# Transposing 64 rows at a time in both halves of the array: a fused windowed-attention and soft-MoE kernel on one Trainium2 core

## The chip, the core and the metric

The kernel runs as one program on one core of a Trainium2 chip. The metric is the device time of one execution, in microseconds (us). The core has five engines that each work through their own instruction queue in order: PE (TensorE: matrix products, with weight loads shown as an engine of their own, PEld), DVE (VectorE), ACT (ScalarE), POOL (GpSimd) and SP (SyncE, which here only issues DMA). PE writes to PSUM, which DVE and ACT read; POOL works on SBUF alone.

## What is computed

Attention with a causal window of 128 positions plus 4 sink positions, then a soft mixture of experts on its output. All data are float32.

```python
# q, k, v: (4 batches, 8 heads, 768 positions, 64)
keep = is_sink | ((rel >= 0) & (rel < 128))          # rel = query position - key position, 4 sinks
a = softmax(where(keep, q @ k.T / 8, -1e9))
x = (a @ v)  laid out as (3072, 512)                 # batch and position, head and dim
logits = x @ phi                                     # (3072, 32): 8 experts of 4 slots
d = softmax(logits, over the 3072 rows)              # dispatch
slot_input = d.T @ x                                 # (32, 512)
slot_out[e] = relu(slot_input[e] @ w1[e]) @ w2[e]    # w1: 512x1024, w2: 1024x512 for each expert
c = softmax(logits, over the 32 slots)               # combine
out = c @ slot_out
```

## The kernel before

**Jobs.** The attention is cut into 12 jobs of 256 positions of one batch (`jobs`: 4 batches, `j` = 0 to 2), all 8 heads at once. Heads lie in pairs: a column block of 128 holds two heads of 64, so `a` = 0 to 3 numbers four pairs, and a "quad" is two pairs. `i` numbers the two blocks of 128 positions of a job, `odd` the two halves of 64 positions in each block. A unit of softmax (`softmax`, `tl` = 0 to 3 in a job) is one quad and one half.

**The steps of a job.** k and q are loaded by DMA (`load`, tile `first_76`) and transposed on PE (`prep`, into `kt` and `qt`). `softmax` makes the scores in tiles of 64x64 of the array into a two-bank PSUM tile `s`; DVE masks and takes the maximum, ACT takes the exponentials into one of three buffers `pts`, POOL divides. `weights_transposed` transposes them into `xws`; `sinks_transposed` does the same for the sink columns. POOL cuts the transposed weights by the window (`select`). `values` multiplies with v into `xt` (features by positions, in `first_77`), `natural` transposes `xt` back to positions by features (`xnb`, also in `first_77`). `Moe.tokens` makes the dispatch logits and adds to the running softmax over rows.

**A transposition** is a product of the data as stationary operand with the identity (`c.ident`): in the profile a weight load (LDWEIGHTS) and a MATMUL `w<-ident,...`. The helper `transpose` does four parts of 128x128 into one PSUM bank, and one copy by ACT or DVE takes the 512 columns out. A job has ten such groups: two for k, two for q, four for the weights and two for `natural`, 40 parts in all.

**PSUM.** There are four single banks of kind `w` (tiles `w` in the profile) and two two-bank tiles of kind `s`.

**Logits.** `tokens` makes them in two steps: `pairs` (four products 32x256 with `phi`, one for each pair of heads, side by side in four column strips of the array), a copy to `lp` (tile `spare`), and `logits` (four products with `c.slot`, which adds the four strips).

**The order of the work** comes from `Plan`: each step is added with a key, the engines that may do it, a guessed time, what it reads and writes, and the shape of array tile it uses (`mode`). `Plan.order` takes for the engine that is free first the ready step with the lowest key, prices a change of mode on PE, and hands out the PSUM banks. The keys come from the table `CFG` (plus 4 for each job). The order is fixed when the program is built; `copy` steps marked "AV" go to ACT or DVE by that same plan. Nearly all instructions of the attention are recorded by one helper, line 127.

**After the attention** comes `finish` (the last steps of the dispatch softmax), then `tail`: the expert products with w1 and w2 (32 weight tiles of 1 MB, 17 of them loaded during the attention, the rest as buffers come free), and the output.

Of the kernel before, what the change touches and what calls it, by code (L numbers as in the profile page):

```python
# [8 lines left out]
F32 = mybir.dt.float32  # L9
# [10 lines left out]
P = 128  # L20
# [120 lines left out]
class Plan:  # L141
# [19 lines left out]
    def add(self, key, eng, time, fn, r=(), w=(), new=None, last=None, mode=(128, 128)):  # L161

        self.steps.append((key, eng, time if isinstance(time, tuple) else (time,) * len(eng), fn,
                           tuple(r), tuple(w), new, last))
        self.modes.append(mode)

    def order(self):
# [3 lines left out]
        for i, (_, eng, _, _, r, w, new, last) in enumerate(steps):  # L171
# [13 lines left out]
            if new is not None:  # L185
                opener[new["name"]] = i
# [17 lines left out]
        while len(order) < len(steps):  # L204
            best = None
            for e, o in todo.items():
                at, t0 = [], 1e9
                for i in o:
                    t = max(free[e], ready[i])
                    new = steps[i][6]  # L210
                    if new is not None:

                        n = len(banks[new["kind"]])
                        if n == 0 or n == 1 and new["kind"] == "w" and not later.get(i, done) <= done:
                            continue
                        t = max(t, min(banks[new["kind"]])[0])
                    at.append((t, i))
                    t0 = min(t0, t)
# [15 lines left out]
            if new is not None:  # L234
                b = min(banks[new["kind"]])
                banks[new["kind"]].remove(b)
                new["bank"] = b[1]
# [12 lines left out]
    def issue(self):  # L250
        order = sorted(self.order())
        end = max(t for t, _, i, e in order if e == "P" and self.steps[i][0] < self.IDLE)
        for t, _, i, e in order:
# [3 lines left out]
            if new is not None:  # L257
                pool, shape, _ = self.pools[new["kind"]]
                new["tile"] = pool.tile(shape, F32, name=new["kind"])
# [18 lines left out]
class Moe:  # L278
# [6 lines left out]
    def __init__(self, nc, c, keep, work, pools, B):  # L285
# [4 lines left out]
        self.spare = keep.tile([P, 256], F32, name="spare")  # L290
# [15 lines left out]
    def tokens(self, plan, keys, b, j, x, xn, blocks):  # L306
# [17 lines left out]
        if both:  # L324

            A, lp = plan.psum(), self.lp
# [6 lines left out]
            plan.add(next(k), "P", 0.45, pairs, r=xs + ["phi"], w=[A["name"]], new=A, mode=(128, 32))  # L333
            plan.add(next(k), "AV", (0.27, 0.34), lambda e: (nc.scalar.copy if e == "A" else nc.vector.tensor_copy)(
                lp, A["tile"][:, 0:256]), r=[A["name"]], w=["lp"], last=A)
# [6 lines left out]
            plan.add(next(k), "P", 0.23, logits, r=["lp"], w=[L["name"]], new=L, mode=(128, 32))  # L342
        else:
            next(k), next(k)

            def logits(e):
                for a in range(4):
                    for g in range(4):
                        nc.tensor.matmul(L["tile"][32 * g:32 * g + 32, 0:P], lhsT=c.phi[:, a, :],
                                         rhs=xt[:, a, x[blocks[0]]], start=(a == 0), stop=(a == 3))  # L350

            plan.add(next(k), "P", 1.2, logits, r=xs + ["phi"], w=[L["name"]], new=L)
# [65 lines left out]
    def finish(self, plan, keys):  # L418
# [11 lines left out]
        swap, slots, sel = self.si.rearrange("p k s -> p (k s)"), self.spare[:, 0:P], self.sel  # L430

        def selectors(e):
            iv, sv = (x.rearrange("p (h i s) -> p h i s", h=2, i=2) for x in (c.ident, swap))
            for i in range(2):
                nc.vector.tensor_copy(sv[:, :, i], iv[:, :, 1 - i])
            nc.vector.reduce_sum(sel, c.ident.rearrange("p (h i s) -> p h s i", h=2, i=2), axis=AX.X)

        plan.add(next(k), "V", 0.6, selectors, w=["fsel"])
# [9 lines left out]
        def inputs(e):  # L448
            for x in range(2):
# [9 lines left out]
        plan.add(next(k), "V", 0.2, lambda e: nc.vector.tensor_copy(  # L459
            slots.rearrange("p (g s) -> p g s", g=4), c.slot.unsqueeze(1).to_broadcast([P, 4, 32])), w=["lp"])  # L460
        plan.add(next(k), "P", 0.25, lambda e: nc.tensor.matmul(Z["tile"][:, 0:1], lhsT=slots, rhs=rz, start=True, stop=True),
                 r=["rz", "lp"], w=["fz"], new=Z)
# [154 lines left out]
class Weights:  # L617
# [9 lines left out]
    def load(self, t):  # L627
# [5 lines left out]
        else:  # L633
# [7 lines left out]
WARM = 8, 10, 24  # L641
PT = 3
CFG = {'prep': [-2.17, -0.88],
       'load': [-3.57, -6.02],
       'v': [-0.18, -0.24],
       'S': -8.73,
       'M': 36.62,
       'E': -5.46,
       'N': 0.31,
       'K0': 2.19,  # L650
       'T': [3.66, 4.85, 4.7, 5.73],
       'K': -1.8,
       'sel': [-6.52, -2.35, 5.2, 5.48],
       'val': [3.28, -5.83, 5.91, 8.36],
       'xn': [2.08, 9.26],
       'tok': [7.72, -14.81, -29.67, 6.11, -4.29, -10.76, 19.93, 9.29, -24.99, 9.79, 6.46, -0.14, -1.55],
       'sm': -17.55,
       'sinks': -36.55,
       'tr': [83.54, 111.89, 84.43, 86.17, 89.04, 123.77, 106.32, 93.21, 89.01, 82.18, 84.62, 87.83, 68.6, 87.87, 106.87,
              85.72, 98.54, 75.2, 46.43, 23.9, 60.71, 53.42, 48.6, 43.21, 70.53, 50.67, 57.49],  # L660
       'w': [14.83, 8.0],
       'fin': [-17.88, 7.56, 0.7, -0.3, 12.51, 20.97, 18.11, 14.38, 20.61, 23.73, 38.59],
       'xn1': [18.28, 18.07],
       'tok1': [4.6, -7.87, -9.73, -4.24, 1.2, -17.1, 3.61, 11.52, -24.18, -0.27, -3.93, 3.34, -6.83]}


def window_path(ctx, tc, c, moe, q, k, v, phi, w1, w2, out):
# [22 lines left out]
    moe.lp = moe.spare[:, 0:256]  # L690
# [21 lines left out]
    QUARTERS, HALVES = (64, 64), (128, 64)  # L712
# [6 lines left out]
    def transpose(key, src, r):  # L719

        h = plan.psum()

        def go(e):
            for a in range(4):
# [22 lines left out]
    def prep(key, n, kind):  # L747

        b, j = jobs[n]
        if kind == 0 and j > 0:  # L750

            add(key, "G", 0.55, lambda e: nc.gpsimd.tensor_copy(ktb[:, :, 0, 4:132], ktb[:, :, 2, 4:132]),
                r=[("kt", 1, 0), ("kt", 1, 1)], w=["kt0"])
        for x in range(2):

            if n == 0:
                h = transpose(key, lambda a, x=x: kqs[kind][:, a // 2, 256 * x + P * (a % 2):256 * x + P * (a % 2) + P],
                              [("kq", kind, i, x) for i in range(2)])
                src, names = "p (i a y) -> p a i y", [(i, x) for i in range(2)]
                a = slice(2 * x, 2 * x + 2)  # L760
                ko, qo = ktb[:, a, 1:3, 4:132], qt[:, a].rearrange("p a (i y) -> p a i y", i=2)
            else:
                h = transpose(key, lambda a, x=x: kqs[kind][:, x, P * a:P * a + P], [("kq", kind, x, y) for y in range(2)])
                src, names = "p (i a y) -> p a i y", [(x, y) for y in range(2)]
                ko, qo = ktb[:, :, 1 + x, 4:132].unsqueeze(2), qt[:, :, P * x:P * x + P].unsqueeze(2)

            def out(e, h=h, src=src, ko=ko, qo=qo):
                s = h["tile"].rearrange(src, i=2 if n == 0 else 1, y=P)
                if kind == 0:
# [457 lines left out]
```

## Time and profile before

| | |
|---|---|
| runs | 257.02, 257.99, 258.00 us; median 257.99 |
| the profiled execution | 257.78 us, with a span of 256.0 us from first to last instruction |
| busy share of the span | PE 89%, PEld 61%, DVE 67%, ACT 56%, POOL 55% |
| granted TensorE clock, mean | 0.964 |
| attention | until 201.12 us, when the first product with w1 starts |
| w1, its transposition, w2 | 201.12 to 232.67 us |
| output | from there to 256.0 us; the last product with the combine weights ends at 243 us |

The first part of the page gives busy time for whole engines over the whole span; the stages differ, so the argument below uses windows of the trace. A PE row gives a start, the time from the first start to the last end, and a count; an fp32 product shows as two MATMULs, a transposition as one.

### The profile page before, as it was taken

How to read it: one execution, taken by the hardware profiler on the slowest of the kernel's cores; microseconds unless marked ns; L12 is line 12 of the kernel's file. 1: busy time of each engine (PE TensorE's matmuls, PEld its weight loads, DVE VectorE, ACT ScalarE, POOL GpSimd, SP SyncE). 2: the span in 40 equal slices, each digit the busy share in tenths (PEclk: the TensorE clock that was granted, in tenths of full speed). 3: DMA queues.
4: the chain of work that ended last, by engine and by line, in shares of the span. 5: the costliest groups of instructions: out<-in, count | busy, mean ns of one | idle time of the engine just before them, and what ended most of it. 6: DMA issues, size and time to landing. Idle time of an engine off the chain costs nothing.

```text
span 256.0 us, 7069 instructions
## 1 busy us (share of the span) xinstructions
PE 229.0 (89%) x2572; PEld 157.2 (61%) x2572; DVE 171.2 (67%) x457; ACT 143.6 (56%) x568; POOL 141.3 (55%) x281
## 2 busy tenths in 40 slices
PE   7778999999999999999999999999699999997800
PEld 7655766776777776676777667677367434345700
DVE  3378968889798979979897997987514513103800
ACT  2367677568596757769675767977615112103700
POOL 1146769587685958669595857869964060000000
PEclk9979999999999999999999999999979999999955
DMA  5699869789899989967999866240609899950995
GB/s 126 133 176 225 227 152 356 186 239 379 162 257 211 343 250 302 276 146 244 256 366 223 235 125 123 59 150 4 206 13 358 300 399 422 414 235 0 399 394 203
DMA packets 84494, 59.34 MB, mean 232 GB/s; under 512 B 76261, under 2 KB 76261, under 8 KB 82917
## 3 DMA queue, kind: packets, MB, share of 16 engines
q1 hardware_dynamic: 84452, 58.83, 76.4%
q8 instruction: 22, 0.36, 0.6%
q14 instruction: 20, 0.16, 0.2%
HBM read 52.53 MB, written 6.29 MB: 230 GB/s over the span
## 4 chain that ended last, share of the span: by engine, by line
PE 66%; DVE 16%; ACT 6%; POOL 5%; issue 3%; ACTq 0%; POOLq 0%; DVEq 0%
PE w L127 47%; PE s L127 17%; DVE wt L127 7%; POOL wt L127 4%; DVE s L127 4%; ACT wt L127 3%; PE w L1179 1%; ACT wt L613 1%; DVE sums L127 1%; DVE first L127 1%; DVE pst L127 1%; DVE spare L127 1%; DVE qt L127 0%; DVE wt L599 0%; ACT wt L598 0%
## 5 line engine op out<-in xcount | busy, mean ns | idle before, releaser
L127 POOL TENSOR_TENSOR wt<-wt 128x528 f32<-128x528 f32 (+1 forms) x96 | 64.3, 673 | 36.3 <-DVE wt L127 22.1
L127 ACT ACTIVATE wt<-s,wt 128x132 f32<-128x132 f32 x192 | 68.8, 386 | 5.6 <-DVE wt L127 5.0
L127 POOL TENSOR_SCALAR_AFFINE_SELECT wt<-wt 128x512 f32<-128x512 f32 x88 | 54.0, 638 | 6.9 <-ACT wt L127 6.4
L127 PE MATMUL w<-wt 128*64 128x128 f32 (+3 forms) x550 | 51.7, 322 | 2.1 <-DVE wt L599 1.5
L127 PE MATMUL s<-wt,qt 64*64 64x196 f32 (+2 forms) x768 | 41.8, 327 | 4.5 <-ACT wt L127 3.7
L127 PEld LDWEIGHTS w<-wt 128*64 128x64 f32 (+2 forms) x550 | 36.7, 143 | 14.8 <-DVE wt L599 2.2
L127 PE MATMUL w<-ident,first 128*128 128x128 f32 x288 | 42.3, 279 | 1.7 <-ACT call L127 1.4
L127 ACT ACTIVATION_READ_ACCUMULATOR wt<-s,wt 128x1 f32 x192 | 42.5, 221 | 0.0
L127 PE MATMUL w<-ident,wt 128*128 128x128 f32 x250 | 38.3, 281 | 1.2 <-POOL wt L127 0.6
L127 PEld LDWEIGHTS w<-ident,first 128*128 128x128 f32 x288 | 32.5, 142 | 7.3 <-issue 2.3
L127 PEld LDWEIGHTS s<-wt,qt 64*64 64x64 f32 x768 | 26.5, 134 | 14.5 <-issue 6.5
L127 DVE TENSOR_REDUCE wt<-s 128x4 f32<-128x528 f32 x48 | 33.9, 707 | 1.7
L127 PEld LDWEIGHTS w<-ident,wt 128*128 128x128 f32 x250 | 28.1, 146 | 11.2 <-issue 3.4
L127 ACT COPY first<-w 128x512 f32<-128x512 f32 x28 | 16.5, 588 | 30.3 <-PE w L127 30.2
L127 ACT COPY wt<-w 128x512 f32<-128x512 f32 x36 | 21.1, 594 | 17.5 <-PE w L127 14.9
L127 DVE COPY_PREDICATED s<-later,s 128x256 f32<-128x256 uint8 x48 | 20.4, 424 | 8.9 <-PE s L127 8.0
L127 DVE COPY wt<-w 128x512 f32<-128x512 f32 x36 | 24.3, 677 | 1.5 <-PE w L127 0.8
L127 DVE COPY first<-w 128x512 f32<-128x512 f32 x20 | 13.7, 684 | 2.0 <-PE w L127 1.9
L127 PE MATMUL w<-wt,si 128*32 128x512 f32 x128 | 13.9, 593 | 0.4 <-DVE si L127 0.4
L127 PE MATMUL s<-wt 128*32 128x512 f32 (+1 forms) x144 | 14.3, 498 | 0.0
L127 DVE MEMSET s<- 64x512 f32 (+1 forms) x16 | 6.2, 385 | 9.5 <-PE s L127 9.1
L127 DVE TENSOR_TENSOR wt<-wt 128x4 f32<-128x4 f32 x48 | 11.2, 232 | 1.8 <-POOL wt L127 0.9
(120 smaller groups left out, 243.9 us busy)
## 6 DMA issues: line engine op xcount, KB each, us to landing
wt<-in_moe_w_dram SPq DMA_DIRECT2D x30, 1024.0 KB, 7.6
wt<-in_v_dram SPq DMA_DIRECT2D x24, 256.0 KB, 3.3
first<-in_q_dram SPq DMA_DIRECT2D x22, 256.0 KB, 3.8
first<-in_k_dram SPq DMA_DIRECT2D x22, 256.0 KB, 4.5
out_dram<-wt SPq DMA_DIRECT2D x5, 1024.0 KB, 5.6
first<-in_moe_w_dram SPq DMA_DIRECT2D x2, 1024.0 KB
out_dram<-wt SPq DMA_DIRECT2D x2, 512.0 KB
first<-in_k_dram SPq DMA_DIRECT2D x4, 128.0 KB, 3.0
```

Source lines behind the costliest of these rows:

```text
L127: return self.tc.keep_in_program_order(f(*args, **kw))
L613: (nc.vector.tensor_copy if i else nc.scalar.copy)(ob[:, n - n0, i], yp)
L1179: nc.tensor.matmul(t[:, 0:P], lhsT=c.ident, rhs=c.ident, start=True, stop=True)
```

## The change

`transpose` now takes eight parts at once and opens two banks. Each part is transposed in two products of 64 rows: rows 0 to 63 in the upper half of the array into the first bank, rows 64 to 127 in the lower half into the second. The stationary operand is 64 rows by 128 columns, the moving one a 64x64 identity. A job has five such units (k, q, the weights of each quad, `natural`) of 16 MATMULs, and again two copies of 512 columns for each. For the very first k and q the units have four parts.

`tokens` makes the logits in one step: 16 products of 32x128 that add up over the four pairs in PSUM. `pairs`, the copy to `lp` and the second product are gone. The units of softmax run quad by quad (`quad, odd = divmod(tl, 2)`), so that the two halves of a quad, which a unit transposes together, follow each other. `Plan` can open several banks for a step. The identity copy for `slots` is made earlier in `finish`. The last filler matmuls (`WARM[2]`) are 64 of 64 columns instead of 24 of 128. All keys of `CFG` have new values.

```diff
-    def transpose(key, src, r):
-        h = plan.psum()
+    def transpose(key, srcs, r):
+        hs = plan.psum(), plan.psum()
         def go(e):
-            for a in range(4):
-                nc.tensor.transpose(h["tile"][:, P * a:P * a + P], src(a), c.ident)
-        add(key, "P", 0.44, go, r=r, w=[h["name"]], new=h)
-        return h
+            for a, src in enumerate(srcs()):
+                for x in range(2):
+                    i = slice(64 * x, 64 * x + 64)
+                    nc.tensor.transpose(hs[x]["tile"][:, 64 * a:64 * a + 64], src[i], c.ident[i, i])
+        add(key, "P", 0.45 if len(r) > 1 else 0.25, go, r=r, w=[h["name"] for h in hs], new=hs, mode=ROWS)
+        return hs
...
-    def weights_transposed(key, n, tl):
-        odd, quad = divmod(tl, 2)
...
-        h = transpose(key, lambda a: pt[:, a, o:o + P], [pn])
...
+    def weights_transposed(key, n, quad):
+        gs = [4 * n + 2 * quad + odd for odd in range(2)]
+        hs = transpose(key, lambda: [pts[g % PT][:, a, o:o + P] for g, o in zip(gs, (0, 4)) for a in range(4)],
+                       [("pt", g % PT) for g in gs])
+        for i in range(2):
+            add(key, *COPY, lambda e, h=hs[i], i=i: copy(
+                e, xws[quad][:, i, 0].rearrange("p h (o y) -> p o h y", o=2),
+                h["tile"].rearrange("p (o h y) -> p o h y", o=2, h=4)),
+                r=[hs[i]["name"]], w=[("xw", quad, i, 0)], last=hs[i])
...
-    def natural(key, n, i):
-        h = transpose(key, lambda a: xt[:, a, P * i:P * i + P], [("xt", i, 0), ("xt", i, 1)])
-        add(key, *COPY, lambda e: copy(e, xnb[i], h["tile"]), r=[h["name"]], w=[("xn", i)], last=h)
+    def natural(key, n):
+        hs = transpose(key, lambda: [xt[:, a, P * i:P * i + P] for i in range(2) for a in range(4)],
+                       [("xt", i, y) for i in range(2) for y in range(2)])
+        for x in range(2):
+            add(key, *COPY, lambda e, h=hs[x], x=x: copy(
+                e, u[:, 0:1024].rearrange("p (i a x y) -> p x i a y", i=2, a=4, x=2)[:, x],
+                h["tile"].rearrange("p (i a y) -> p i a y", i=2, a=4)), r=[hs[x]["name"]], w=[("xn", x)], last=hs[x])
...
-            def pairs(e):
-                for a in range(4):
-                    nc.tensor.matmul(A["tile"][32 * a:32 * a + 32, 0:256], lhsT=c.phi[:, a, :], rhs=xt[:, a, :],
-                                     start=True, stop=True)
...
-            def logits(e):
+        def logits(e):
+            for a in range(4):
                 for g in range(4):
-                    nc.tensor.matmul(L["tile"][32 * g:32 * g + 32, 0:P], lhsT=c.slot, rhs=lp[:, x[g % 2]],
-                                     start=True, stop=True)
+                    nc.tensor.matmul(L["tile"][32 * g:32 * g + 32, 0:P], lhsT=c.phi[:, a, :],
+                                     rhs=xt[:, a, x[g % 2 if both else blocks[0]]], start=(a == 0), stop=(a == 3),
+                                     skip_group_check=True)
...
-        odd, quad = divmod(tl, 2)
+        quad, odd = divmod(tl, 2)
...
-WARM = 8, 10, 24
+WARM = 8, 10, 64
...
-       'xn': [2.08, 9.26],
+       'xn': [-7.99],
```

In the order of the built programs, PE between two score steps of a middle job before (`first_76` holds k and q, `first_77` holds `xt` and `xnb`, `wt` after `ident` is the softmax weights or, twice, the sinks):

```order
L127 MATMUL s<-wt,qt 64x196 x8
L127 MATMUL w<-ident,wt 128x128 x4
L127 MATMUL w<-ident,first_77 128x128 x4
L127 MATMUL w<-ident,wt 128x128 x6
L127 MATMUL w<-ident,first_77 128x128 x4
L127 MATMUL w<-first_77,phi 32x256 x4
L127 MATMUL w<-ident,wt 128x128 x4
L127 MATMUL w<-ident,first_76 128x128 x4
L127 MATMUL w<-spare,slot 32x128 x4
L127 MATMUL s<-wt,qt 64x196 x16
```

All four-part groups here run in one mode of the array, 128x128, with the sinks among them. PE in the changed kernel, around the logits of a middle job:

```order
L127 MATMUL w<-ident,first_76 128x64 x16
L127 MATMUL w<-ident,first_77 128x64 x16
L127 MATMUL w<-first_77,phi 32x128 x16
L127 MATMUL w<-ident,wt 128x64 x16
L127 MATMUL s<-wt,qt 64x196 x16
L127 MATMUL w<-ident,wt 128x128 x2
L127 MATMUL w<-ident,first_76 128x64 x16
L127 MATMUL w<-ident,lt 128x128
L127 MATMUL w<-pst,vsink 128x256 x2
```

Groups of four parts have become units of 16 MATMULs of half the columns; the sinks and the one transposition of `lt` now stand alone in the 128x128 mode, and the two products of the logits, with other work between them before, are one block.

A second place on PE is the last job of a batch in the changed kernel, where the dispatch weights of `tokens` are turned (`lt`) and used (`lb`):

```order
L127 MATMUL s<-wt,qt 64x196 x8
L127 MATMUL w<-ident,wt 128x64 x16
L127 MATMUL w<-ident,wt 128x128 x2
L127 MATMUL w<-ident,lt 128x128
L127 MATMUL w<-first_77,lb 32x256 x4
L127 MATMUL s<-wt,qt 64x196 x8
```

Here `lb` follows `lt` at once. Before, 12 or 16 transpositions stood between the two in the middle jobs:

```order
L127 MATMUL w<-ident,lt 128x128
L127 MATMUL w<-ident,first_76 128x128 x12
L127 MATMUL w<-ident,wt 128x128 x4
L127 MATMUL w<-first_77,lb 32x256 x4
L127 MATMUL w<-pst,vsink 128x256 x2
```

Now nothing stands between them once in three jobs; in the other two jobs a product with v and a score step do.

More of the change, by code (lines that the diff above doesn't have):

```diff
@@ L184, in order @@
             before.append(d)
-            if new is not None:
-                opener[new["name"]] = i
+            for x in new:
+                opener[x["name"]] = i
             for x in r + w:
@@ L233, in order @@
                 todo[x].remove(i)
[L234 to L237, printed above, removed]
+            for x in new:
+                b = min(banks[x["kind"]])
+                banks[x["kind"]].remove(b)
+                x["bank"] = b[1]
             free[e] = end = t0 + times[engs.index(e)]
@@ L323, in tokens @@
         xs = [("xt", b, u) for b in blocks for u in range(2)]
[L324 to L352 removed]
+        def logits(e):
+            for a in range(4):
+                for g in range(4):
+                    nc.tensor.matmul(L["tile"][32 * g:32 * g + 32, 0:P], lhsT=c.phi[:, a, :],
+                                     rhs=xt[:, a, x[g % 2 if both else blocks[0]]], start=(a == 0), stop=(a == 3),
+                                     skip_group_check=True)
+        plan.add(next(k), "P", 0.87, logits, r=xs + ["phi"], w=[L["name"]], new=L, mode=(128, 32))
         key = next(k)
@@ L435, in selectors @@
                 nc.vector.tensor_copy(sv[:, :, i], iv[:, :, 1 - i])
+            nc.vector.tensor_copy(slots.rearrange("p (g s) -> p g s", g=4),
+                                  c.slot.unsqueeze(1).to_broadcast([P, 4, 32]))
             nc.vector.reduce_sum(sel, c.ident.rearrange("p (h i s) -> p h s i", h=2, i=2), axis=AX.X)
-        plan.add(next(k), "V", 0.6, selectors, w=["fsel"])
+        plan.add(next(k), "V", 0.8, selectors, w=["fsel"])
         mm = [("m", 0), ("m", 1)]
@@ new lines, in prep, with out @@
+            hs = transpose(key, src, [("kq", kind, i, y) for i in range(2) for y in quads])
+            for x in range(2):
+                def out(e, h=hs[x], x=x, heads=heads, m=256 * len(quads)):
+                    s = h["tile"][:, 0:m].rearrange("p (i a y) -> p i a y", i=2, y=64)
+                    o = 64 * x
+                    if kind == 0:
+                        copy(e, ktb[:, heads, 1:3, 4 + o:68 + o].rearrange("p a i y -> p i a y"), s)
+                        return
+                    t = qt[:, heads].rearrange("p a (i x y) -> p x i a y", i=2, x=2)[:, x]
+                    if e == "A":
+                        nc.scalar.mul(t, s, D ** -0.5)
+                    else:
+                        nc.vector.tensor_scalar(t, s, D ** -0.5, None, op0=ALU.mult)
+                add(key, "AV", (0.52, 0.65) if n else (0.32, 0.4), out, r=[hs[x]["name"]],
+                    w=[("q" if kind else "kt", x, y) for y in quads], last=hs[x])
@@ L787, in softmax @@
+            if kind == 0 and j == 0:
+                add(key, "G", 0.25, lambda e, a=heads: nc.gpsimd.tensor_copy(
+                    ktb[:, a, 1:3, 0:4], ktb[:, a, 1:2, 4:8].to_broadcast([P, a.stop - a.start, 2, 4])),
+                    r=[("kt", 0, y) for y in quads], w=[("kts", 0, y) for y in quads])
     def softmax(keys, n, tl):
@@ L889, in select @@
         prev, cur = xws[quad][:, i, 0], xws[quad][:, i, 1]
[L890 removed]
+        pn = [("xw", quad, i, 0)]
         add(key, "G", 0.57, lambda e: nc.gpsimd.affine_select(
@@ L974, in window_path @@
         end = "1" if n == N - 1 else ""
-        for i in range(2):
-            natural(t(O["xn" + end][i]), n, i)
+        natural(t(O["xn" + end][0]), n)
         moe.tokens(plan, [t(x) for x in O["tok" + end]], b, j, half, xnb, (0, 1))
@@ L999, in window_path @@
     for quad in range(2):
-        add(100.0, "D", 3.0, lambda e: weight(), w=[("xw", quad, i, 1) for i in range(2)] + [
-            ("xw", quad, i, 0, x) for i in range(2) for x in range(2)])
+        add(100.0, "D", 3.0, lambda e: weight(), w=[("xw", quad, i, x) for i in range(2) for x in range(2)])
     for n in range(9):
```

138 lines of the change are left out of this document (53 added, 85 removed).

## Prediction

> **What bounds the kernel now.** I read the busy shares first, then the table of windows, then the waits of each engine in the steady part.
>
> ```profile
> span 256.0 us, 7069 instructions
> PE 229.0 (89%) x2572; PEld 157.2 (61%) x2572; DVE 171.2 (67%) x457; ACT 143.6 (56%) x568; POOL 141.3 (55%) x281
> ```
>
> To find the steady period I took the first product with `phi` of two jobs nine jobs apart, and the window between them (busy us of PE, PEld, DVE, ACT, POOL).
>
> ```profile
> 39.26 0.42 PE L127 MATMUL w<-first,phi 128*32 128x256 f32 x4
> 170.30 0.42 PE L127 MATMUL w<-first,phi 128*32 128x256 f32 x4
> 39.26:170.30 131.04, 128.92 (x1588) 93.09 (x1584) 114.84 (x297) 93.11 (x390) 96.90 (x184) 1.00 0.85 237
> ```
>
> 131.04 / 9 = 14.56 us for a job, in which PE is busy 14.32, DVE 12.76, ACT 10.35, POOL 10.77. PE is idle 0.24 us a job, and its only rows in the list of waits for that window (us in all, times, longest) are the first two here; the longest of DVE and ACT follow:
>
> ```profile
> PE w L127 <- ACT call L127: 1.4, 3, 0.5
> PE w L127 <- DVE wt L127: 0.5, 1, 0.5
> ...
> DVE s L127 <- PE s L127: 9.7, 16, 1.2
> ...
> ACT first L127 <- PE w L127: 21.6, 13, 2.5
> ```
>
> DVE waits for scores and ACT for products, both from PE. So the attention is bound by PE, and a shorter PE job shortens the kernel as long as DVE, at 12.76 of 14.56, can follow. After the attention nothing that the change touches is left:
>
> ```profile
> 201.12 13.94 PE L127 MATMUL w<-wt,si 128*32 128x512 f32 x128 [0.38 <-DVE si L127]
> 235.96 8.21 SPq L614 DMA_DIRECT2D out_dram<-wt  x7
> ```
>
> 55 us from the first row to the end of the span stay as they are.
>
> **Transpositions, the main term.** What a group costs on PE is read from start to start:
>
> ```profile
> 66.18 0.89 PE L127 MATMUL s<-wt,qt 64*64 64x196 f32 x16
> 67.01 0.66 PE L127 MATMUL w<-ident,wt 128*128 128x128 f32 x4
> 67.50 0.60 PE L127 MATMUL w<-ident,first 128*128 128x128 f32 x4
> 67.94 0.82 PE L127 MATMUL w<-ident,wt 128*128 128x128 f32 x6
> 68.59 0.60 PE L127 MATMUL w<-ident,first 128*128 128x128 f32 x4
> 69.12 0.64 PE L127 MATMUL w<-first,phi 128*32 128x256 f32 x8
> 69.69 0.66 PE L127 MATMUL w<-ident,wt 128*128 128x128 f32 x4
> 70.18 0.60 PE L127 MATMUL w<-ident,first 128*128 128x128 f32 x4
> 70.71 0.43 PE L127 MATMUL w<-spare,slot 128*32 128x128 f32 x8
> 71.07 1.56 PE L127 MATMUL s<-wt,qt 64*64 64x196 f32 x32
> ```
>
> Inside one mode four transpositions take 0.44 us (67.50 to 67.94), so 0.109 for one, or 0.85 ns a column. 40 parts a job cost 4.36 us. The scores row shows what array halves are worth: 16 products of 196 columns at 0.85 ns would be 2.67 us one after the other; 66.18 to 67.01 is 0.83 with the change of mode. So four 64x64 tiles stream at once, two of them row halves, and the new form should run its two halves at once too. A pair then streams 64 columns, 64 x 0.85 = 0.055 us. Each product also needs its own weight load of 128 columns, and the question is whether that fits:
>
> ```profile
> L127 PEld LDWEIGHTS w<-ident,first 128*128 128x128 f32 x288 | 32.5, 142 | 7.3 <-issue 2.3 <-ACT call L127 2.1 <-DVE wt L127 1.3
> L127 PEld LDWEIGHTS w<-first,phi 128*32 128x32 f32 x96 | 1.9, 108 | 2.1 <-issue 1.0 <-ACT wt L127 0.5 <-ACT first L127 0.3
> L127 PEld LDWEIGHTS w<-lt,acc 128*128 128x128 f32 x4 | 0.5, 190 | 0.0
> ```
>
> An ordinary load of 128 columns takes 190 ns, one of 32 columns 108: 82 ns for 96 columns, again 0.85 ns a column, so 109 ns for 128 and a fixed part of 81. A load for a transposition takes 142, so its columns take about 61 ns. The pitch of a pair is the larger of 55 and 61. Bounds: 55 if the load hides wholly, 109 if a 64-row load goes at the ordinary rate or the two halves load in turn (122). I take 60, since the row is that of a transposition. A unit of eight pairs: 0.48 us against 8 x 0.109 = 0.87; five units: 5 x 0.39 = 1.95 us saved a job.
>
> The Trainium skill ("TensorE: Matmul & The Clock Gate", section "LDWEIGHTS (loading the stationary operand)") says that a load takes its columns divided by 1.2 per ns and that the rows don't matter: 107 ns for 64 rows by 128 columns. By that rule a unit would take 8 x 107 = 0.86 us and nothing is saved. The trace agrees for ordinary loads (109) and not for those of transpositions (61).
>
> **Changes of mode.** 69.12 to 69.69 is 0.57 for two rounds of 256 columns, 0.44 by 0.85 ns; 70.71 to 71.07 is 0.36 for 0.22. So a change costs about 0.14 us. Counted over three middle jobs in the order, there were 39 and are now 44: +5/3 x 0.14 = +0.23 us a job.
>
> **Logits.** Before: 0.44 + 0.22 = 0.66 us of streaming. Now 16 products, two MATMULs each, four at a time: 8 rounds of 128 columns, 0.87. +0.21 a job. The copy goes from the vector engines:
>
> ```profile
> L127 DVE COPY spare<-w 128x256 f32<-128x256 f32 x10 | 4.1, 413 | 0.0
> L127 DVE COPY wt<-w 128x512 f32<-128x512 f32 x36 | 24.3, 677 | 1.5 <-PE w L127 0.8
> L127 ACT COPY wt<-w 128x512 f32<-128x512 f32 x36 | 21.1, 594 | 17.5 <-PE w L127 14.9 <-PE s L127 2.5
> ```
>
> **PE sum.** 14.32 - 1.95 + 0.23 + 0.21 = 12.81 us a job, -1.51.
>
> **Can the others follow?** The copies keep number and size (512 columns, 677 on DVE and 594 on ACT), but the new order gives DVE 47 instead of 65 of the large ones and no `spare`, ACT 93 instead of 79. DVE loses 18 x 0.677 + 10 x 0.413 = 16.3 us in all and takes 2.3 of small copies from ACT, ACT gains 14 x 0.594 = 8.3 and gives up 1.4: DVE 11.6, ACT 10.9, POOL 10.8 a job. At a period of 13.2 DVE is at 88%, as it is now, but ACT goes from 71% to 83% and POOL from 74% to 82%. PE will wait more often. One place is sure: where `lb` follows `lt` at once. The last such chain shows its length (PE, then ACT, then PE):
>
> ```profile
> 185.49 0.33 PE L127 MATMUL w<-ident,lt 128*128 128x128 f32 x1 [1.91 <-ACT lt L127]
> 185.85 0.21 ACT L127 COPY lb<-w 128x64 f32<-128x64 f32 x1 [0.42 <-PE w L127]
> 186.12 0.88 PE L127 MATMUL w<-first,lb 128*32 128x256 f32 x8
> ```
>
> 0.63 from start to start, less the 0.11 of the transposition: 0.5 bare, once in three jobs, 0.17 a job. A unit now needs two of four banks at once and both copies before they are free; I add 0.15 a job for that, between nothing (now hidden) and 0.3 at each of five units (half a copy). Idle goes from 0.24 to 0.56: period 13.37, -1.19 us a job, 12 jobs -14.3.
>
> **The ends.** The last job's chain loses `pairs`, copy and second product (0.57 + 0.4 + 0.36 with waits about 1.4) and gets one block (0.87 + 0.14): -0.4 to -0.8. At 187 us PE ran slow after an idle stretch, which the window of these 8 us (granted clock 0.79, the third number from the end) and the same work 3 us later show:
>
> ```profile
> 184.00:192.00 8.00, 6.43 (x53) 4.23 (x55) 1.75 (x4) 1.92 (x7) 5.47 (x14) 0.79 0.07 18
> 187.65 2.99 PE L127 MATMUL w<-wt 128*64 128x256 f32 x24
> 191.01 1.96 PE L127 MATMUL w<-wt 128*64 128x256 f32 x24
> ```
>
> The fillers may now cover it (-1.0) or not; I count -0.3. Costed at nothing: the DMAs keep their number, size and place (17 weight tiles between the loads of the jobs), and a load of q or k lands in 3.8 or 4.5 us (last column) and is needed a job later:
>
> ```profile
> first<-in_q_dram SPq DMA_DIRECT2D x22, 256.0 KB, 3.8
> first<-in_k_dram SPq DMA_DIRECT2D x22, 256.0 KB, 4.5
> ```
>
> If SP held one up, PE would wait at the next unit of k, at most some 4 us once. The earlier `slots` copy lies on DVE beside a PE that is still in the attention. Sum: 257.8 - 14.3 - 0.9 = 242.6; the profiled execution and the median of the runs (257.99) are 0.2 apart. I say 242.5 us.
>
> **Rivals.** *The weight load sets the pitch* (the other side). If a 64-row load runs at 109 ns, a unit takes 0.87 as before, and the job gains 0.44 us of PE work from modes and logits: 12 x 0.44 = +5.3, less 0.9 at the end, 262; with the two halves in turn, at 122, 12 x (0.44 + 0.52) - 0.9 gives 268. It decides from a pitch of (4.36 - 0.44) / 40 = 98 ns a pair upward. For it: `w<-lt,acc`, the only row with 128 columns of weights to 64 of moving, has the full 190. Against: that is no transposition, and 288 transpositions have 142. The rule of the Trainium skill named above ("TensorE: Matmul & The Clock Gate") leads here: by its 107 ns the time would be 261, an estimate.
>
> *The vector engines become the bound.* DVE and ACT together were busy 23.1 of 29.1 us a job, 79%. If waiting on each other holds them to 80%, the 22.5 us that are left need a period of 14.06, -0.5 a job: 12 x 0.5 + 0.9 gives 251; with 82% it is 13.7 and 247. For it: POOL waits for DVE and ACT already, and two banks come free later than one. Against: DVE alone stands at 88% now with PE full. The Trainium skill ("TensorEngine Tiling (Array Packing)", section "PSUM Bottleneck") says that array tiles speed up TensorE but not the copies out of PSUM, which may become the limit.
>
> *PE stays as full as it is.* Idle 0.24 or less, no cold clock: 12 x 1.51 + 2 gives 237.5.
>
> **Chances.** My forecast, 238 to 247: 0.62. Vector engines, 247 to 256: 0.21. PE as full as now, under 238: 0.09. The weight load, 258 to 268: 0.08. Leaving out the last, and the far part of the two others, the range is 236.5 to 250.5; the likeliest case's own is 238 to 247. A change of 0.5% (1.3 us) is about what a measurement can tell here. Faster by more 0.90, within it 0.03, slower 0.07.
>
> **What the new profile would show.** Units of 16 MATMULs that take 0.48 us from start to start in one mode, 0.62 with a change; a unit of 0.9 or more proves the first rival. The period between products with `phi` near 13.4 us and DVE no longer the fuller of the two by 2.4 us. PE's idle time near 0.5 us a job: over 1 us proves the second rival. The first product with w1 near 186 us and 55 us behind it; if the tail is longer than that, weight tiles came late, and I was wrong about the DMAs.

## The result, and the profile after

The changed kernel takes 251.59 us (median of four runs, 251.42 to 251.75); the kernel before, in the same rounds, 258.0 us. The ratio is 0.9759, with a 95% interval of 0.9734 to 0.9784: 6.4 us faster, where 15.5 were forecast, and 1.1 us above the range. The profiled execution took 251.75 us.

The head of its page, to set beside the one of before:

```profile
span 250.0 us, 8413 instructions
PE 215.5 (86%) x3260; PEld 150.6 (60%) x3260; DVE 161.1 (64%) x440; ACT 151.0 (60%) x577; POOL 141.9 (57%) x281
```

PE and DVE have each lost 3% of the span, ACT and POOL have gained 4 and 2%: the whole span does not tell what bounds the kernel. The timeline of PE shows that the new operations have the length that was forecast:

```profile
33.88 0.71 PE L127 MATMUL w<-ident,first 64*128 64x64 f32 x16
34.52 0.50 PE L127 MATMUL w<-pst,vsink 128*128 128x256 f32 x2
...
80.05 1.08 PE L127 MATMUL w<-first,phi 128*32 128x128 f32 x32
81.06 0.89 PE L127 MATMUL s<-wt,qt 64*64 64x196 f32 x16
```

A unit of eight parts takes 0.64 us from its start to the next one's, with the change of mode (forecast 0.62), and the logits 1.01 (0.87 + 0.14). Within a unit the two halves of a pair start 3 ns apart, by the starts of the single MATMULs, and pairs follow each other every 62 ns.

The windows of the trace (time, then busy us of PE, PEld, DVE, ACT, POOL; the granted clock is the third number from the end): nine jobs between two products with `phi`, as in the prediction, and then one batch, job by job.

```profile
38.52:164.43 125.91, 117.89 (x2107) 86.04 (x2104) 104.77 (x279) 101.29 (x404) 96.83 (x182) 1.00 0.90 246
80.05:96.00 15.95, 14.37 (x259) 10.35 (x255) 11.10 (x32) 12.44 (x51) 14.95 (x29) 1.00 1.00 289
96.00:109.25 13.25, 11.98 (x212) 8.93 (x208) 11.50 (x31) 11.16 (x45) 9.07 (x19) 1.00 0.89 251
109.25:122.20 12.95, 12.95 (x243) 9.42 (x240) 12.37 (x33) 10.34 (x41) 8.56 (x16) 1.00 1.10 241
```

The period is 125.91 / 9 = 13.99 us a job instead of 14.56 (forecast 13.37). PE is busy 13.10 (forecast 12.81) and idle 0.89 (forecast 0.56), DVE 11.64, ACT 11.25, POOL 10.76. The three jobs of a batch differ: 15.95, 13.25, 12.95, and the next batch repeats that to within 0.1.

The rows of PE in that batch that have an idle time before them (in brackets, with what ended it):

```profile
83.36 0.90 PE L127 MATMUL s<-wt,qt 64*64 64x196 f32 x16 [0.77 <-ACT wt L127]
86.47 0.64 PE L127 MATMUL w<-first,lb 128*32 128x256 f32 x8 [0.57 <-DVE lb L127]
98.86 0.89 PE L127 MATMUL s<-wt,qt 64*64 64x68 f32 x16 [0.76 <-ACT wt L127]
108.61 0.71 PE L127 MATMUL w<-ident,first 64*128 64x64 f32 x15 [0.51 <-ACT first L127]
```

Two of the four wait for exponentials to free a score tile, one is the bare `lt` to `lb`, and one is a unit that waits for an ACT copy of `xt`. Together they are 2.6 us of a batch of 42.15.

PE is idle in 6% of the time, then. What the other 94% hang on, the chain of waits of the same batch tells: followed back from its last instruction, at each step to what released it (start, length, engine and tile):

```profile
80.00 0.60 DVE wt L127
...
86.28 0.14 DVE lb L127
...
86.47 0.64 PE w L127 x8
87.12 0.90 PE s L127 x16
88.01 5.93 PE w L127 x82
93.94 0.86 PE s L127 x14
```

From 80.0 to 86.4 the chain runs on DVE without a break; from 86.47 to 94.8 it is PE alone. Its shares from 80 to 123 us, about one batch, in the kernel before and in the changed one (the view cuts its line off there):

```profile
by line: PE w L127 60.6%; PE s L127 17.3%; DVE wt L127 6.9%; DVE s L127 5.0%; ACT wt L127 3.5%; issue 2.4%; DVE sums L127 1.5%; DVE first L127 1.4%; DVE spare L127 0.8%; DVE pst L127 0.8%; ACT call L127 0.3%; ACT lb L127 0.2%; ACTq L127 0.1
```

```profile
by line: PE w L127 23.4%; DVE wt L127 22.4%; ACT wt L127 15.0%; DVE s L127 13.4%; PE s L127 9.6%; issue 4.8%; DVE rs L127 3.3%; DVE first L127 2.5%; DVE call L127 1.4%; ACT first L127 1.1%; DVE acc L127 1.1%; DVE sums L127 1.1%; ACT pst L12
```

The chain lay on PE for 78% before, and lies on it for 33% now. Even before it left PE once in a batch, from 95.2 to 105.0 us, for DVE and ACT. PE in that stretch of the kernel before, two of its rows and the window:

```profile
97.32 0.64 PE L127 MATMUL w<-first,phi 128*32 128x256 f32 x8
...
99.54 1.56 PE L127 MATMUL s<-wt,qt 64*64 64x132 f32 x32
95.22:105.02 9.80, 9.29 (x110) 6.85 (x110) 9.13 (x24) 7.29 (x34) 8.43 (x15) 1.00 1.06 308
```

PE counts as busy for 9.29 of the 9.80 us, but the five groups from `phi` to the next scores take 2.22 us there (97.32 to 99.54), where the same five in the prediction's rows take 1.95 (69.12 to 71.07): busy time holds short waits.

Two windows of the changed kernel, the first the stretch on PE alone, the second the one that leads up to the same place of the next batch:

```profile
86.47:94.96 8.49, 8.48 (x138) 6.32 (x140) 3.96 (x12) 6.73 (x26) 8.23 (x17) 1.00 1.08 306
114.19:128.62 14.43, 12.86 (x237) 8.87 (x233) 13.82 (x40) 12.65 (x54) 10.87 (x20) 1.00 0.91 221
```

In the first PE is full and DVE half idle. In the second DVE is busy 96% and ACT 88%, and PE has 1.6 us to spare. The mean of 83% for DVE over nine jobs hides both.

Behind the attention:

```profile
195.34 13.94 PE L127 MATMUL w<-wt,si 128*32 128x512 f32 x128
```

The first product with w1 starts at 195.34 instead of 201.12, and 54.7 us follow (54.9 before). Where the time went, from the starts of the products with `phi`: the first job -0.74 us, the next nine jobs -5.13, the last two jobs +0.80 (24.21 instead of 23.41), the chain behind them -0.71 (6.70 instead of 7.41).

### The profile page after: what moved, and what is told of

Read it like the earlier page. It is cut to its first block, busy times and chain, and to the rows that moved or that the text cites. A ratio compares the mean times of both kernels' runs of the same rounds, so it can differ in the third digit from the quotient of the medians.

```text
span 250.0 us, 8413 instructions
## 1 busy us (share of the span) xinstructions
PE 215.5 (86%) x3260; PEld 150.6 (60%) x3260; DVE 161.1 (64%) x440; ACT 151.0 (60%) x577; POOL 141.9 (57%) x281
## 4 chain that ended last, share of the span: by engine, by line
PE 52%; DVE 26%; ACT 13%; issue 4%; POOL 1%; ACTq 0%; DVEq 0%; POOLq 0%
PE w L127 34%; PE s L127 16%; DVE wt L127 12%; ACT wt L127 10%; DVE s L127 8%; DVE rs L127 2%; PE w L1158 2%; ACT wt L594 1%; DVE first L127 1%; DVE call L127 1%; ACT first L127 1%; DVE acc L127 1%; DVE sums L127 0%; POOL wt L127 0%; ACT qt L127 0%
## 5 line engine op out<-in xcount | busy, mean ns | idle before, releaser
L127 POOL TENSOR_TENSOR wt<-wt 128x528 f32<-128x528 f32 x96 | 63.8, 670 | 19.4 <-DVE wt L127 6.0
L127 PE MATMUL w<-ident,wt 64*128 64x64 f32 (+1 forms) x442 | 29.2, 241 | 2.9 <-ACT wt L127 1.1
L127 ACT COPY wt<-w 128x512 f32<-128x512 f32 (+1 forms) x41 | 23.7, 581 | 11.4 <-PE w L127 8.4
L127 PEld LDWEIGHTS w<-ident,wt 64*128 64x128 f32 (+1 forms) x442 | 21.6, 144 | 12.3 <-issue 5.5
L127 DVE COPY wt<-w 128x512 f32<-128x512 f32 (+1 forms) x33 | 22.0, 667 | 10.5 <-PE w L127 10.5
L127 PEld LDWEIGHTS w<-ident,first 64*128 64x128 f32 x576 | 22.2, 143 | 10.9 <-issue 5.1
L127 PE MATMUL w<-ident,first 64*128 64x64 f32 x576 | 27.4, 234 | 1.5 <-ACT first L127 1.5
L127 DVE TENSOR_TENSOR wt<-wt 128x4 f32<-128x4 f32 x48 | 13.6, 284 | 10.2 <-ACT wt L127 9.0
L127 ACT ACTIVATE qt<-w 128x512 f32<-128x512 f32 (+1 forms) x25 | 14.4, 580 | 6.8 <-PE w L127 4.9
L127 POOL COPY wt<-wt 128x512 f32<-128x512 f32 (+2 forms) x13 | 5.7, 455 | 13.4 <-ACT wt L127 10.9
```

The costliest lines, as they stand in the source:

```text
L127: return self.tc.keep_in_program_order(f(*args, **kw))
```

## The experiments

All are compared with the kernel before, in the same rounds. The start of the kernel differs from run to run (its first product with `phi` stands at 37.0 to 41.6 us where the first job is the same), which makes the intervals wide; so I also give the length of one steady batch, from the fourth to the seventh product with `phi`, which mostly repeats to 0.1 us: 42.15 in the changed kernel, 43.86 before.

### What the two halves of the array are worth

```diff
-                    i = slice(64 * x, 64 * x + 64)
+                    i = slice(0, 64)
                     nc.tensor.transpose(hs[x]["tile"][:, 64 * a:64 * a + 64], src[i], c.ident[i, i])
```

> Leaves out one half of the transposed data: both products of a part read rows 0 to 63, so that the two MATMULs of a pair are in the same half of the array and cannot stream at once; number of instructions, order, copies and banks are those of the changed kernel. If the two halves are what shortens a unit, a unit goes from 0.50 us (pairs every 62.5 ns) to about 1.0 us (16 products of 55 to 62 ns), 2.4 us a job. PE sets the time: 251.6 + 12 x 2.4 = 280 us, or 270 if PE's 0.89 us of idle time a job takes up the first of it. If the pitch came from the weight loads alone (16 loads, whatever half), nothing changes: 251.6.

270.12 us, ratio 1.0514 (1.042 to 1.0608); a batch takes 46.75 us.

```profile
90.09 1.21 PE L127 MATMUL w<-ident,first 64*128 64x64 f32 x16
91.22 0.89 PE L127 MATMUL s<-wt,qt 64*64 64x196 f32 x16
```

The unit now takes 1.13 us with its change of mode, 0.49 more than 0.64. So the halves run at once, and the main term of the prediction holds. The time rose by 18.5 us for 60 x 0.49 = 29 us of work: more than a third of it went into time in which PE had not been what the kernel waited for.

### Less work for PE alone

```diff
-            for a in range(4):
+            for a in range(2 if n else 4):
                 for g in range(4):
                     nc.tensor.matmul(L["tile"][32 * g:32 * g + 32, 0:P], lhsT=c.phi[:, a, :],
```

> Leaves out half of the 16 products of the logits (two of four head pairs) in jobs 1 to 11: PE has 4 rounds of 128 columns less, 0.44 us a job, and all else is the same. Theory A, PE sets the time and its idle time stays what the order makes it: 11 x 0.44 = 4.8 less, 247. Theory B, DVE and ACT together (22.9 us of 28.0 a job) set the period and PE's 0.89 us of idle time is their slack: 0 to 1 less, 251.

251.42 us, ratio 0.9795 (0.973 to 0.9861): nothing. Its windows:

```profile
80.20:96.16 15.96, 14.02 (x244) 9.92 (x240) 11.10 (x32) 12.45 (x51) 14.96 (x29) 1.00 0.99 285
96.16:109.40 13.24, 11.70 (x195) 8.64 (x192) 11.50 (x31) 11.16 (x45) 9.06 (x19) 1.00 0.92 257
109.40:122.33 12.93, 12.59 (x227) 9.02 (x224) 12.34 (x33) 10.33 (x41) 8.56 (x16) 1.00 1.02 247
```

Each job has PE 0.3 to 0.4 us shorter and the same length to 0.02 us, also the third, where PE had been busy 12.95 of 12.95. A PE that is full in the profile was not the limit at these three places. Theory A, on which the forecast rests, falls for them.

### Less work for ACT and DVE

Two of the four exponentials of a unit (`range(2 if n else 4)` around the activations):

> Leaves out two of the four exponentials of each softmax unit in jobs 1 to 11: ACT has 4 x 2 x 0.345 = 2.8 us a job less and frees the score tile 0.7 us earlier. Theory A: only the waits of PE for a score tile go (3.8 us in nine jobs, 0.42 a job), 11 x 0.42 = 4.6 less, 247. Theory B: DVE and ACT have 20.1 instead of 22.9 us a job and PE becomes the bound at 13.1: 11 x 0.89 = 9.8 less, 242.

254.48 us, ratio 0.9879 (0.9751 to 1.0006). In this kernel the clock fell to half once more in the middle, so that the total says little. The profile shows that in one window (0.90) and not in the batch behind it:

```profile
97.13:138.90 41.77, 39.77 (x705) 29.28 (x701) 36.05 (x94) 26.50 (x87) 32.70 (x62) 1.00 0.93 241
79.83:97.13 17.30, 16.09 (x259) 11.26 (x256) 11.38 (x32) 9.35 (x31) 14.97 (x29) 0.90 0.94 278
```

The undisturbed batch takes 41.77, 0.38 us less than 42.15 for 7.4 us less work on ACT (26.50 instead of 33.94). Neither theory expected so little: ACT is not the pace, and the tile that it frees earlier helps only a little.

Half of the columns of a unit's copies, in all of them, in those on DVE, and in those on ACT:

```diff
-            add(key, *COPY, lambda e, h=hs[i], i=i: copy(
-                e, xws[quad][:, i, 0].rearrange("p h (o y) -> p o h y", o=2),
+            add(key, *COPY, lambda e, h=hs[i], i=i, m=1 if n else 2: copy(
+                e, xws[quad][:, i, 0].rearrange("p h (o y) -> p o h y", o=2)[:, 0:m],
...
```

> Copies only half of the columns out of PSUM for every unit of transpositions in jobs 1 to 11 (256 instead of 512 columns, ten copies a job): DVE and ACT have about 10 x 0.27 = 2.7 us a job less, almost as much as with half the exponentials, but the chain from scores to exponentials is as long as it was. Theory A: the named waits shrink a little where an exponential or lb stands behind a copy, 0.1 to 0.3 a job, 248 to 250.5. Theory B: PE becomes the bound, 242.

> Copies only half of the columns of a transposition unit where the copy is on DVE (37 copies of jobs 1 to 11, each 0.68 to 0.42 us: 9.8 us less work on DVE); copies on ACT stay whole. Theory D, formed after the first four runs: in each batch of three jobs DVE is full for some 34 of 42 us and sets the pace there, PE only in the other 8. Then most of the gain of half_copies (4.5 us) is here: 247 to 248. Theory E, the two engines together as one pool, or ACT: 9.8 of the 25 us that half_copies took away are here, so 1.8 less, 250, or nothing.

> The reverse: half of the columns where the copy of a unit is on ACT (73 copies of jobs 1 to 11, 0.59 to 0.38 us: 15.3 us less work on ACT), copies on DVE whole. Theory D: ACT is not the pace: 0 to 1 less, 250.6 to 251.6. Theory E (one pool, or ACT): 2.7 to 4.5 less, 247 to 249.

All: 247.09 us, 0.9649 (0.9568 to 0.973), a batch of 41.19. DVE's alone: 250.03, 0.9713 (0.9669 to 0.9757), 42.03. ACT's alone: 250.53, 0.9735 (0.9692 to 0.9779), 42.04. So the two parts bring 0.1 us a batch each and both together 1.0. I read that as the other engine's copies being next where one's become shorter; no run shows it. It is against theory D as I had put it (DVE alone) and against theory E's 247 to 249 for ACT's part, and DVE's part even made one job longer: 15.36 for 15.95 in the first job of a batch, but 13.62 for 13.25 in the second.

The mask, which DVE does ahead of each maximum:

```diff
-            nc.vector.copy_predicated(own if odd else old, where(odd), old if odd else own)
+            if n == 0:
+                nc.vector.copy_predicated(own if odd else old, where(odd), old if odd else own)
```

> Leaves out the masking instruction of DVE (128x256, 0.424 us) in each softmax unit of jobs 1 to 11: 44 x 0.424 = 18.7 us less on DVE, nothing else. Theory D: DVE falls from 11.64 to 9.9 us a job, and PE becomes the pace with its 13.1: 0.8 us a job less, 242 to 244. Theory A (PE waits for the chain from scores to exponentials): only the 0.42 us a job in which PE waits for a score tile, 247. If POOL sets the long job: 251.

246.05 us, ratio 0.9585 (0.9524 to 0.9646), a batch of 40.38: between the 247 of theory A and the 242 to 244 of theory D.

```profile
78.48:93.71 15.23, 14.37 (x259) 10.35 (x255) 9.51 (x27) 12.09 (x49) 14.29 (x27) 1.00 1.04 279
93.71:105.96 12.25, 11.70 (x212) 8.69 (x208) 10.56 (x27) 11.10 (x45) 9.33 (x19) 1.00 1.05 303
105.96:118.86 12.90, 12.90 (x243) 9.36 (x240) 11.36 (x30) 10.74 (x42) 9.10 (x18) 1.00 1.08 249
```

This is the largest effect, 1.77 us a batch, in the first two jobs. The mask lies on DVE and also in the path from scores to maximum to exponentials to the next scores, whose steps lie on three engines; this run does not tell the one from the other. Without the masks the chain of such a batch lies on PE for 76% again (58.1% for the tiles `w`, 17.8% for `s`). PE is left idle 0.47 us a job (40.38 - 38.97 = 1.41 in three), about what I had forecast for the whole change.

### POOL

```diff
-            pt, pt, z.unsqueeze(2).to_broadcast([P, 4, 132]), op=ALU.mult)
+            pt[:, 0:m], pt[:, 0:m], z[:, 0:m].unsqueeze(2).to_broadcast([P, m, 132]), op=ALU.mult)
```

> POOL divides only two of the four weight blocks of each softmax unit in jobs 1 to 11 (528 to 264 elements, 1.07 to about 0.55 us): 44 x 0.5 = 22 us less on POOL. In the long job of a batch (15.95 us) POOL is 94% busy. If POOL sets it: the long jobs fall to about 13.2 as the others, 4 x 2.7 = 11 less, 241. Theory D: within 1 of 251.6.

252.36 us, ratio 0.9775 (0.9707 to 0.9844); the total is disturbed by its start (first product with `phi` at 41.6 us), a batch takes 41.44. POOL, 94% busy in the long job, does not set it alone: that job falls from 15.95 to 15.24, not to 13.2, as much as without the masks. And POOL's shorter divisions made DVE's own work shorter, 33.83 us a batch instead of 34.97, of which 0.44 is in the rows of the last section; so this run does not tell POOL from DVE.

### The start

```diff
+        for _ in range(8):
+            nc.tensor.matmul(h["tile"][:, 256:384], lhsT=c.ident, rhs=c.ident, start=True, stop=True, ...)
```

> The changed kernel with 8 more filler products of 128 columns behind the product for the sinks at about 13 us, where PE otherwise waits 1.95 us; their bank's other half, no other step is moved. PE's granted clock is half for 10.24 us from 17.25 us on, 3.4 us in the kernel before. If that idle stretch brings the half clock: first logits at 36 to 37 us instead of 38.5, 249 to 250. If the start is set by the chain through ACT and DVE, or the half clock comes anyway: 251.6.

251.99 us, ratio 0.9759 (0.9723 to 0.9795): nothing. Windows of the changed kernel, then of this one:

```profile
16.00:20.00 4.00, 3.36 (x54) 2.34 (x46) 2.98 (x11) 2.02 (x10) 2.40 (x5) 0.66 1.06 189
20.00:24.00 4.00, 2.02 (x27) 1.54 (x24) 3.85 (x9) 3.33 (x16) 2.96 (x5) 0.50 0.66 143
24.00:28.00 4.00, 3.66 (x42) 2.37 (x44) 1.85 (x6) 0.65 (x2) 3.20 (x8) 0.56 1.24 231
```

```profile
20.00:24.00 4.00, 1.23 (x24) 0.95 (x24) 3.85 (x10) 3.39 (x16) 2.97 (x5) 0.81 0.68 144
24.00:28.00 4.00, 3.50 (x34) 2.07 (x34) 1.83 (x5) 0.58 (x1) 3.37 (x8) 0.50 1.15 206
28.00:32.00 4.00, 3.29 (x55) 2.60 (x52) 2.73 (x7) 3.72 (x18) 1.47 (x2) 0.84 0.59 127
```

The half clock came later and was shorter (0.38 + 1 + 0.32 of 4 us, 6.8 us instead of 10.2), and the first logits still stood at 38.98 us instead of 38.52. From 20 to 24 us DVE is busy 3.85 of 4 in both: there too PE follows.

### Did the pace pass from PE to the vector engines?

The same two edits in the kernel before: the mask left out, and the products with the preceding block of v (`if j > 0` in `values`) left out.

> The kernel before, with the same masking instruction left out in jobs 1 to 11 (44 x 0.424 = 18.7 us less on DVE). In the changed kernel that took 5.5 us. Theory D (before, PE sets the pace and DVE has slack; the change has handed the pace to the chain through DVE): at most PE's idle time, 0.24 us a job, 0 to 2.6 less, 255.5 to 258. If DVE was a limit before as well: 5 less, 253.

> The kernel before, without the products of the softmax weights with the preceding block of v (8 MATMULs of 128 columns for each quad of the eight jobs with j > 0; a quad's block takes 1.45 instead of 1.89 us): 8 x 0.87 = 7.0 us less on PE, nothing else. Theory D: PE sets the pace before, so nearly all of it shows: 251 to 252. If the time is set elsewhere, as in the changed kernel where 4.8 us less on PE changed nothing: 257 to 258.

253.28 us, ratio 0.9797 (0.9742 to 0.9852), and 252.31 us, 0.9766 (0.9735 to 0.9797). By the totals the second is close to what theory D expected. The first is not: masks were worth 2% in the kernel before too, where PE was busy 98%. The steady batch of the kernel before, without the masks, and without these products:

```profile
82.58:126.44 43.86, 43.30 (x534) 31.17 (x533) 38.73 (x101) 31.53 (x134) 32.56 (x62) 1.00 0.91 258
```

```profile
82.30:125.17 42.87, 42.66 (x534) 31.20 (x533) 34.66 (x89) 31.30 (x134) 32.41 (x62) 1.00 0.96 262
```

```profile
81.13:124.31 43.18, 41.81 (x502) 29.51 (x501) 38.66 (x101) 31.46 (x134) 32.47 (x62) 1.00 0.93 262
```

Without the masks a batch is 0.99 us shorter. The stretch from 95.2 to 105.0 us, where the chain had left PE, held two masks of 0.43 us. Of the 0.99, 0.64 was counted as busy PE, with the same 534 MATMULs. Without the products PE is busy 1.49 us less and the batch 0.68 shorter: in the steady part, less than half of PE's work counted even before the change.

The edit of `values` in the changed kernel:

> The changed kernel without the products of the softmax weights with the preceding block of v, the same 7.0 us less work on PE that took 5.6 us from the kernel before. Theory D (in the order of the changed kernel the pace is a chain through DVE and ACT, and PE has slack): 0 to 2 less, 249.6 to 251.6. If PE still sets the pace as before the change: 5 to 6 less, 246.

248.9 us, ratio 0.9677 (0.962 to 0.9733): between the two theories, and 0.8% below the changed kernel, where the same edit took 2.3% from the kernel before (each ratio is known to 0.3 or 0.6%). The traces do not bear that difference out. The batch is 41.26 us, 0.89 shorter for 1.51 less of busy PE, against 0.68 for 1.49 before; and the first product with w1 starts 4.06 us earlier, against 4.56. So what speaks for a pace that has passed on is the chain's share on PE (78% to 33%) and the masks' worth in a batch (0.99 to 1.77 us), not these totals.

```profile
78.92:93.99 15.07, 13.49 (x243) 9.46 (x240) 10.88 (x32) 12.34 (x51) 14.23 (x28) 1.00 1.02 294
93.99:107.24 13.25, 11.36 (x195) 8.13 (x191) 11.50 (x31) 11.18 (x45) 9.78 (x20) 1.00 1.00 275
```

The windows also tell where PE sets the pace in the changed kernel. The products left out lie in the first and the second of them. The first, which holds the stretch of 8.5 us with PE full, falls by 0.88, one for one (PE is busy 0.88 less); the second keeps 13.25 with PE 0.62 shorter.

### Another order

```diff
-       'S': -10.57,
-       'M': 2.63,
+       'S': [-9.63, 9.63, 12.43, 52.82],
+       'M': [36.6, -19.46, 34.94, 41.41],
...
-        add(keys["M"], "V", 1.1 + (0.55 * (1 - odd) + 0.15) * (j == 0), maxima, r=[sn], w=[sn, nn])
+        add(keys["M"], "V", 1.1 + (0.77 * (1 - odd) + 0.4) * (j == 0), maxima, r=[sn], w=[sn, nn])
```

> The changed kernel with new keys for the order (those of the softmax steps apart for the four units of a job), found against guessed times that were set to what the trace shows (mask and maximum of a batch's first job 2.27 and 1.5 us instead of 1.8 and 1.25, slot softmax sums 1.3 instead of 0.7, a unit 0.5 instead of 0.45); no step is left out. If the forecast's missing microseconds lie in the order (waits for the chain through DVE and ACT, the last two jobs): 245 to 248. If DVE's and ACT's load cannot be arranged better: 250 to 252.

245.75 us, ratio 0.9562 (0.9496 to 0.9627): the fastest kernel here that leaves nothing out, below both others.

```profile
80.06:94.55 14.49, 13.39 (x243) 9.86 (x239) 12.90 (x33) 11.67 (x48) 11.48 (x22) 1.00 0.88 246
94.55:107.81 13.26, 13.20 (x243) 9.82 (x239) 12.45 (x32) 10.78 (x45) 10.55 (x19) 1.00 0.94 257
107.81:121.26 13.45, 12.47 (x227) 9.15 (x223) 12.32 (x31) 11.21 (x46) 10.76 (x20) 1.00 0.84 221
```

A batch takes 41.20, and the work of the jobs is spread more evenly. The first product with w1 starts at 188.89, 6.45 us earlier than in the changed kernel: 1.96 of these are won up to the tenth product with `phi`, and 4.49 behind it: 4.69 in the last two jobs, the place where the change had lost 0.8, less 0.2 in the chain behind them. The kernel before was not given new keys in this way, so it is open how much of this gain needs the change.

> The same edit in the retuned order (245.75). If the new order has given the pace back to PE: 4 to 6 less, 240 to 242. If DVE, now 12.5 us a job of 13.7, sets it: 0 to 2 less, 244 to 245.75.

> The retuned kernel without the masking instruction in jobs 1 to 11 (18.7 us less on DVE). PE is idle 0.71 us a job in its steady part. If PE sets the pace: that idle time at most, and what lies in the start, 2 to 6 less, 240 to 244; if DVE sets it: 8 or more less, under 238.

243.43 us, ratio 0.9489 (0.9426 to 0.9553), a batch of 41.19: PE's relief, 1.5 us a batch by PE's busy time (39.06 to 37.56), changes nothing there; the total lies between the two expectations, since the start became 0.95 us shorter and the last two jobs 1.03. 243.27 us, ratio 0.9447 (0.938 to 0.9513), a batch of 39.77: the masks bring 1.43. That total lies in the range that I had set for PE, but PE's own relief speaks against it. In the steady batch the new order has not given the pace back to PE; it has made the ends shorter and the vector engines' work more even.

## Why the prediction was wrong

- **The transposition's price** was right: 62 ns a pair, 0.64 us for a unit with its change of mode against 0.62; the rival of the weight load is refuted, and `same_half` shows the halves' worth. In that run a product with its own load of 128 columns followed every 62 ns ((1.13 - 0.14) / 16) in one half. The rule of the Trainium skill ("TensorE: Matmul & The Clock Gate", "LDWEIGHTS (loading the stationary operand)"), 107 ns for 128 columns, does not hold for these loads.
- **Logits and modes** were right, 1.01 us for the block.
- **PE's work** of 12.81 us a job was measured as 13.10. The windows account for about 0.1 of the 0.29: the one of after holds 64.0 starts of score MATMULs a job, the one of before 62.2, which is one score step of 0.83 us in nine jobs. Five units at 0.64 instead of 0.62 are another 0.1; the rest is open.
- **The step that failed** is the one after that: "the attention is bound by PE, and a shorter PE job shortens the kernel as long as DVE, at 12.76 of 14.56, can follow". I took PE's 98% as proof that PE alone set the pace and its 0.24 us of idle time as all its waiting, and then added two small waits, 0.32 us a job, for what the others would cost. Already in the kernel before busy PE time held waits for a chain on DVE and ACT, 1.49 us less work on PE shortened a batch by 0.68 only, and masks on DVE counted 0.99. In the changed kernel PE became 1.22 us a job shorter and the period 0.57. The chain lies on PE for a third of a batch. In one stretch of 8.5 us of 42 PE's work counts one for one (`no_prev`); where it was left out elsewhere, in the logits of the three jobs of a batch (`half_logits`) and in the second job's products with v, it counted nothing. For the rest the chain runs over scores, mask and maximum, exponentials and copies, on DVE and ACT by turns, with DVE at 96% in its fullest stretch. The period was 13.99 for 13.37, which is 0.62 x 9 = 5.6 us of the nine that are missing.
- **The rival that came true** is the second, the vector engines, which forecast a period of 14.06 and 251 us from 80% for DVE and ACT together. They were busy (104.77 + 101.29) / (2 x 125.91) = 82%. That it met the time is in part luck: by its own sum 82% gives 247, the vector engines had 22.9 us of work a job and not 22.5, and 3.2 us were lost in the last two jobs, which it did not foresee. Its own sign, over 1 us of idle PE a job, was missed at 0.89. What I held against it was a mean, DVE at 88% before with PE full; the mean was the wrong number, since the stretches differ. The page of the Trainium skill that I had named there ("TensorEngine Tiling (Array Packing)", "PSUM Bottleneck") pointed the right way, and the trace agrees as far as the copies go: halved, they bring 1.0 us a batch, while the masks bring 1.77.
- **The last two jobs** were counted with the steady saving, 2 x 1.19 us; they took 0.8 longer, 3.2 us off. A period was carried to a place with another mix of work. `retuned` shows that this was the order and no limit: there they are 4.69 us shorter.
- **The first job** saved 0.74 instead of 1.19, and **the chain at the end** 0.71 of 0.9. The tail of 55 us and the DMAs stayed as said.

Open is what share of the masks' worth is DVE's load and what is the length of the path from scores to scores, and what sets the steady batch of the new order, where the products with v that PE does count nothing and the masks 1.43 of 41.20 us.

## What to carry to other kernels

An engine at 98% in the profile is the pace only if less work on it shortens the time: an edit that leaves out a piece of its work, with all else in place, tells it in one run, and the chain of waits over one period hints at it beforehand: it had left PE for ten of 44 us in a stretch where PE counted as busy. When the fullest engine gets faster, cut the period into stretches and look for the one in which the next engine is already full; means over a period with uneven jobs hide it. And an order that was fitted to guessed durations should be fitted again when the trace shows others: here that, with more keys to set, was worth nearly as much as the change itself (5.8 and 6.4 us).

## What the hardware did that I had not expected

**A DVE instruction of six elements took as long as POOL's division beside it.** The instruction on the tile `rs` in the kernel before, and in the changed one, with the timeline of both engines there (count, then least, median and greatest duration in ns, first and last start):

```profile
L127 DVE TENSOR_SCALAR rs<-rs x4: 171/172/173, 78.1 to 202.6; 128x6 f32<-128x6 f32 x4
```

```profile
L127 DVE TENSOR_SCALAR rs<-rs x4: 172/965/966, 78.4 to 196.8; 128x6 f32<-128x6 f32 x4
```

```profile
78.42 0.96 DVE L127 TENSOR_SCALAR rs<-rs 128x6 f32<-128x6 f32 x1
...
78.29 1.06 POOL L127 TENSOR_TENSOR wt<-wt 128x528 f32<-128x528 f32 x1 [1.13 <-DVE wt L127]
```

The two instructions end together, at 79.38 and 79.35, and with half the division (`half_divide`) the small one takes 526 ns (median), 0.44 us less. The Trainium skill ("SBUF — State Buffer", "SBUF: two separate sides") says that DVE, in some of its instructions, and GpSimd share a pair of ports as an exclusive lock, held for a whole instruction; the trace agrees. The new order had put the two side by side in three of the four batches, 0.8 us of DVE where the chain ran on it.

**Half clock in whole pieces.** Windows of the kernel before, at its start:

```profile
12.00:16.00 4.00, 1.48 (x20) 0.97 (x20) 3.35 (x12) 3.35 (x17) 1.74 (x3) 0.96 0.99 195
16.00:20.00 4.00, 3.81 (x31) 3.26 (x32) 2.85 (x8) 2.14 (x11) 2.07 (x6) 0.61 0.78 143
```

That is (0.04 + 0.39) x 2 x 4 = 3.4 us of half clock. In the changed kernel it was (0.34 + 0.50 + 0.44) x 8 = 10.2, with the fillers 6.8: one, three and two times the same piece. The Trainium skill ("TensorE: Matmul & The Clock Gate", "Part 1: The HAM clock gate (the "warmup" mystery)") tells of windows of some 3.4 us in which the activity is watched; the trace agrees. How long the half clock lasts does not by itself tell when the first product with `phi` starts, in kernels whose first job is the same: with 10.2 us of it that was at 37.0 us (`half_copies`) and 38.5 (the changed kernel), with 6.8 at 38.7 (`half_logits`), and with 20.5 at 41.6 (`half_divide`).
